# Splitting queries and keys before they are turned, and turning them by DMA, in a fused attention and expert kernel

## The chip, the cores and the metric

The kernel runs on one core of a Trainium2 chip. The metric is the device time of one execution in microseconds (us), the median of several runs. TensorE is called PE, VectorE DVE, ScalarE ACT, GpSimd POOL; SP is the queue from which every DMA of this kernel is issued.

## The reference

Attention with queries averaged in pairs (32 heads, 1,152 keys and 576 queries each, width 64), then a layer over 2,304 tokens:

```python
q_pool = q.reshape(B, H, S // 2, 2, D).mean(axis=3)          # B, H, S, D = 4, 8, 1152, 64
scores = np.matmul(q_pool, k.transpose(0, 1, 3, 2)) / np.sqrt(D)
attn = np.exp(scores - scores.max(-1, keepdims=True))
attn = attn / (attn.sum(-1, keepdims=True) + 1e-09)
x = np.matmul(attn, v)                                       # then heads beside each other: 2304 x 512
h = x @ w_in                                                 # 512 x 1024, inputs in float64
sm = softmax(h); solu = h * sm
ln = (solu - mean) / np.sqrt(var + 1e-06) * g_ln
out = ln @ w_out                                             # 1024 x 512
```

## The kernel before

Every factor of a product is split into a float16 high part and a float16 low part, and the products of the parts are added in PSUM. Heads are taken in 16 pairs P; a head g has nine steps, each 128 keys against all 576 queries, 288 steps in all. A step is two score products for each half of the queries (`q,w` and `q,w2h` in the trace; pair 0 works in float32, `q,w2f`), an exponential on ACT, and the product with the values, five matmuls of 128 queries by 65 columns for each pair of parts. `eh` holds the exponentials' high part; a second exponential on ACT in float32 (`e32`, `e` in the trace) and a subtraction on POOL (`rest`, line 1104) give the low part beside it. For steps that the table `EX` picks (`whole`), ACT writes float32 alone, nothing is subtracted, and the five matmuls take float32 exponentials and float32 values (`vx`): one matmul in the program, two in the trace.

Ahead of a head's steps, `maxima` (line 944) multiplies queries by keys once more in 128 x 384 pieces, and DVE reduces each piece (`mx`, line 960) to find the shift of the exponentials.

`pair` (line 600) brings in queries, keys and values of a pair. Before the change PE turns nine 128 x 128 blocks of keys (`kt`, line 716) and five of queries (`qt`, line 802) per pair; ACT writes the high part from PSUM (`khi`, `q`), DVE the low part (`klo`, `q`, line 444, from PSUM); then plain DMAs put high and low parts beside each other (`k_put`, line 733; `q_beside`, line 823). The two expert weights come in 16 parts of 128 x 512, read as 64-bit words and made into float32 by ACT, POOL and DVE (`weight_part`), and split by `weight_split`: high on ACT, low on DVE (`wil`, `wol`). From step 78 on, 18 tiles of 128 tokens go through `tokens` (line 1234) between the steps.

The order on each engine is that of a planner (`Plan`): each operation is handed in with a wanted time `at`, counted in steps, an engine and a length; `run` plays these through and fixes the order. The numbers in `KP` set the wanted times and which steps take which path.

## Time and profile before

| | |
|---|---|
| median of 3 runs (lowest to highest) | 713.29 us (713.26 to 714.19) |
| the profiled execution: its time / its span | 713.3 us / 711.5 us |
| mean granted clock of PE | 0.97 |
| busy: PE / DVE / ACT / POOL | 651.9 / 561.8 / 560.7 / 491.0 us |
| HBM read / written | 36.70 / 4.72 MB |

Busy time is the union of an engine's spans; a matmul's span is longer than the distance to the next one, so what a matmul costs PE is read from start to start. The first scores start near 22.6 us of the span, head 2 near 67.4, head 4 near 100.3, head 8 near 180.3, head 9 near 201.5, and head 31 near 614.1.

### The profile page before, as it was taken

The numbers are of one execution on the slowest core, as the hardware profiler recorded it, in microseconds if no ns is written. First come the engines' busy times: TensorE is split into PE (matmuls) and PEld (weight loads), VectorE is DVE, ScalarE is ACT, GpSimd is POOL, SyncE is SP. The second block draws the span as 40 slices with busy tenths as digits, with TensorE's granted clock in tenths as the row PEclk, the third lists the DMA queues.
The fourth block names the chain that finished last, engine by engine and source line by source line (L and its number), as shares of the span: only waits on it lengthen the run. The fifth ranks groups of instructions, "written<-read, shape, count | busy, mean of one in ns | idle before, by whom it ended". The sixth has DMA issues, their size and how long they took to land.

```text
span 711.5 us, 19079 instructions
## 1 busy us (share of the span) xinstructions
PE 651.9 (92%) x7109; PEld 458.7 (64%) x7109; DVE 561.8 (79%) x1421; ACT 560.7 (79%) x1346; POOL 491.0 (69%) x643
## 2 busy tenths in 40 slices
PE   8879898677788999999999999999999999999995
PEld 7767676556555666676666666667767666665542
DVE  6689999998998888888888778797888786445551
ACT  3768789778879898899888887898989887864432
POOL 3575769776787978788878887778778787840100
PEclk9889999879989999999999999999999999999998
DMA  6664645442333333323423241423242201010101
GB/s 180 146 169 117 171 114 132 127 115 74 90 78 85 76 86 93 82 62 111 93 75 84 78 99 52 117 60 95 72 101 74 70 11 25 17 23 16 28 17 30
DMA packets 81048, 59.52 MB, mean 84 GB/s; under 512 B 64572, under 2 KB 64572, under 8 KB 80956
## 3 DMA queue, kind: packets, MB, share of 16 engines
q1 hardware_dynamic: 80956, 58.31, 32.5%
q8 instruction: 55, 0.90, 0.5%
q14 instruction: 37, 0.30, 0.1%
HBM read 36.70 MB, written 4.72 MB: 58 GB/s over the span
## 4 chain that ended last, share of the span: by engine, by line
PE 39%; DVE 10%; ACT 6%; issue 2%; POOL 2%; ACTq 0%; POOLq 0%; DVEq 0%
PE bank L438 35%; DVE mx L960 3%; PE bank L1343 2%; ACT e L1081 2%; DVE q L444 2%; ACT eh L1081 2%; ACT q L812 1%; POOL eh L1104 1%; DVE e L1293 1%; ACT e L1286 1%; DVE st L1274 1%; PE bank L1254 1%; PE bank L716 1%; POOL st L1326 1%; DVE e L1330 0%
## 5 line engine op out<-in xcount | busy, mean ns | idle before, releaser
L1104 POOL TENSOR_TENSOR eh<-e,eh 128x512 f16<-128x512 f32 (+1 forms) x491 | 394.2, 828 | 117.0 <-ACT e L1087 30.6
L960 DVE TENSOR_REDUCE mx<-bank 128x1 f32<-128x384 f32 x420 | 219.1, 547 | 35.0 <-PE bank L438 33.3
L1081 ACT ACTIVATE e<-bank 128x288 f32<-128x288 f32 x426 | 177.1, 428 | 10.0 <-POOL eh L1104 5.5
L1081 ACT ACTIVATE eh<-bank 128x288 f16<-128x288 f32 x384 | 160.1, 425 | 29.4 <-PE bank L438 27.0
L438 PE MATMUL bank<-q,w 128*128 128x288 f16 (+1 forms) x576 | 165.6, 296 | 5.4 <-ACT e L1087 2.5
L438 PEld LDWEIGHTS <-eh 128*128 128x128 f16 x3924 | 142.5, 100 | 19.4 <-issue 7.7
L438 PE MATMUL bank<-q,w2h 65*128 65x288 f16 x540 | 153.3, 292 | 0.0
L438 PE MATMUL bank<-w,q 128*128 128x384 f16 (+1 forms) x390 | 122.1, 336 | 32.7 <-DVE mx L960 16.4
L438 PE MATMUL bank<-vhi,eh 128*128 128x65 f16 x2544 | 143.8, 197 | 1.8 <-DVE x L1160 1.7
L438 PE MATMUL bank<-vlo,eh 128*128 128x64 f16 x1380 | 140.8, 196 | 0.0
L438 PEld LDWEIGHTS <-w 128*128 128x128 f16 x540 | 53.5, 99 | 46.0 <-issue 20.7
L438 PEld LDWEIGHTS <-w2h 65*128 65x128 f16 x540 | 53.3, 99 | 40.8 <-issue 13.3
L1087 ACT ACTIVATE eh<-bank 128x576 f16<-128x576 f32 (+1 forms) x75 | 48.8, 657 | 11.8 <-PE bank L438 11.5
L438 PEld LDWEIGHTS <-q 128*128 128x128 f16 x360 | 35.4, 100 | 29.8 <-DVE q L444 7.7
L1326 POOL TENSOR_TENSOR st<-st 128x1 f32<-128x1 f32 x54 | 11.6, 215 | 60.4 <-ACT junk L1313 58.6
L444 DVE SCALAR_TENSOR_TENSOR q<-bank,qs,q 64x192 f16<-64x192 f32 (+2 forms) x120 | 38.7, 362 | 12.2 <-ACT q L812 8.6
L1087 ACT ACTIVATE e<-bank 128x576 f32<-128x576 f32 x63 | 41.4, 658 | 0.7 <-DVE eh L1104 0.4
L812 ACT ACTIVATE q<-bank,qs 64x384 f16<-64x384 f32 (+2 forms) x60 | 29.8, 496 | 6.6 <-PE bank L802 4.2
L1274 DVE TENSOR_REDUCE st<-bank 128x1 f32<-128x512 f32 x36 | 24.7, 685 | 11.3 <-PE bank L438 10.8
L719 ACT ACTIVATE khi<-bank,qs 128x384 f16<-128x384 f32 x45 | 27.2, 604 | 4.8 <-PE bank L716 3.6
L438 PE MATMUL bank<-wil,xh 128*128 128x512 f16 x104 | 30.7, 378 | 0.0
L438 PE MATMUL bank<-wih,xh 128*128 128x512 f16 x104 | 30.6, 384 | 0.0
(167 smaller groups left out, 1160.6 us busy)
## 6 DMA issues: line engine op xcount, KB each, us to landing
qt<-in_q_dram SPq DMA_DIRECT2D x16, 576.0 KB
kt<-in_k_dram SPq DMA_DIRECT2D x32, 288.0 KB
vt<-in_v_dram SPq DMA_DIRECT2D x14, 576.0 KB
out_dram<-o SPq DMA_DIRECT2D x36, 128.0 KB
w<-khi SPq DMA_DIRECT2D x30, 144.0 KB
w<-klo SPq DMA_DIRECT2D x30, 144.0 KB
w2h<-w SPq DMA_DIRECT2D x30, 144.0 KB
raw<-in_moe_w_in_dram SPq DMA_DIRECT2D x8, 511.6 KB
```

The lines of the kernel that those rows point to most:

```text
L438: nc.tensor.matmul(out=o, lhsT=a, rhs=b, start=first, stop=last, skip_group_check=True)
L444: nc.vector.scalar_tensor_tensor(out=o, in0=a, scalar=scale, in1=b, op0=ALU.mult, op1=ALU.subtract)
L716: nc.tensor.transpose(ps[:, c, :], tl["kt", P][:, 3 * i + c].rearrange("p h d -> p (h d)"), ident)
L719: nc.scalar.activation(out=tl["khi", P][:, 3 * i:3 * i + 3], in_=tl["kps", (P, i)], func=ACTF.Copy, scale=tl["qs", P][:, 2:3])
L812: nc.scalar.activation(out=tl["q1", P][r, :, t, :], in_=ps, func=ACTF.Copy, scale=tl["qs", P][r, 1:2])
L960: nc.vector.tensor_reduce(out=tl["mx", g][:, m, c:c + 1], in_=tl["nps", (g, m, c)], op=ALU.max, axis=AXX)
L1081: nc.scalar.activation(out=tl[name, (g, j)][:, f * HALF:(f + 1) * HALF], in_=tl[tn(j, f), (g, j, f)], func=ACTF.Exp, scale=esc,)
L1087: nc.scalar.activation(out=new((name, (g, j)), [128, SQ * 4 // mybir.dt.size(dtype)], dtype)[:, 0:SQ].rearrange("p (f i) -> p f i", f=2), ...
L1104: eng.tensor_tensor(out=e[:, o:o + c.stop - c.start], in0=e32[:, c], in1=e[:, c], op=ALU.subtract)
L1274: nc.vector.tensor_reduce(out=st(f), in_=tl[H_[f]], op=ALU.max, axis=AXX)
L1326: nc.gpsimd.tensor_tensor(out=st(o), in0=st(a), in1=nhalf if b is None else st(b), op=op)
L1343: nc.tensor.transpose(ps[:, c, :], tl[E][:, o:o + 128], ident)
```

## The change

Queries and keys of pairs 1 to 15 are split as they lie, in SBUF: ACT writes the high part, DVE the low part, into one tile in which high and low alternate (`kn`) or in two (`qa`, in which POOL copies the high part a second time beside itself, and `qb`). Six DMA transposes per pair, two of 128 x 1152 and four of 64 x 1152 float16, bring the turned parts where the products want them. The PE transposes, the reads of PSUM and the plain DMAs that set parts beside each other are gone; a plain DMA copies the high keys of each head to `khi`. The weights' first product writes to PSUM, and their low part is formed against a copy of the high part that PE puts into PSUM (`ups`); the float32 weights and their two parts share a tile. All values are loaded into two fixed float32 tiles. `EX` goes from 12 float32 steps (steps 10 to 34) to 31, every second one from 10 to 70. `OFF` adds an offset to the wanted time of each operation, and `KP` has new numbers.

```diff
-KP = {'W': [2, 4.42, 4.58], 'step': 1.32, 'M': [78.27, 16.0, 7.69], 'TX': 115, 'TP': 75, 'win': 5.1, 'P': [25.14, 18.81, 12.42, 24.66, 30, 23.73], 'QP': 27, 'N': [11.54, 7], 'AV': 4.37, 'CD': [[19, 71, 1], [71, 283, 10]], 'SD': [[11, 74, 2], [79, 283, 0]], 'VM': 'BBCCACBCBACCABBA', 'AH': 8, 'OF': [4.15, 1.91, 9.71, 2.05, 1.96], 'N1': 10.15, 'warm': 1, 'ws': 1.98, 'GR': 1, 'GG': 19, 'b_eh': 6, 'b_w1': 4, 'V0': -54.65, 'VF': 1, 'QD': [0, 1], 'L0': 0.56, 'F': 0, 'EX': [[10, 36, 47]], 'LX': [0, 23.98], 'HP': [146073, 0], 'DL': 2000, 'MA': 17.97, 'WS': [50, 75, 1.36]}
+KP = {'W': [2, 4.44, 4.7], 'step': 1.05, 'M': [78.33, 15.88, 7.65], 'TX': 118, 'TP': 69, 'win': 4.28, 'P': [24.74, 18.81, 12.81, 18.34, 35, 22.83], 'QP': 29, 'N': [11.98, 7], 'AV': 5.18, 'CD': [[27, 53, 2], [69, 288, 10]], 'SD': [[12, 83, 5], [70, 287, 1]], 'VM': 'BACCBCACBCCBCACB', 'AH': 8, 'OF': [4.76, 1.62, 9.84, 2.47, 1.86], 'N1': 8.51, 'warm': 1, 'ws': -3.83, 'GR': 0, 'GG': 13, 'b_eh': 6, 'b_w1': 4, 'V0': -98.83, 'VF': 1, 'QD': [0, 1], 'L0': 2.74, 'F': 0, 'EX': [[10, 71, 50], [42, 282, 0]], 'LX': [3, 36.19], 'HP': [146073, 0], 'DL': 2000, 'MA': 18.0, 'TR': [2000, 2], 'P1': [-3.89, -3.14, 3.71, -7.84, -10.1, 0.03], 'WS': [47, 70, 0.22], 'KD': 5.48, 'KL': 0, 'WP': 0}
+OFF = {'am.0': -3.59, 'am.1': 4.37, 'am.10': -9.61, 'am.11': -5.09, 'am.12': -8.44,
...
+        at += OFF.get(self.group((writes or reads)[0]), 0)
...
-    tag(1, "kt")
+    tag(2, "kt")
...
         def product():
+            ps = psum(("wps", n), WN)
             nc.vector.tensor_scalar(
-                out=w32.bitcast(I32), in0=tl["raw", n][:, :, 0], scalar1=5, scalar2=128 << 23,
+                out=ps.bitcast(I32), in0=tl["raw", n][:, :, 0], scalar1=5, scalar2=128 << 23,
                 op0=ALU.logical_shift_right, op1=ALU.bitwise_or,
             )
-            nc.vector.tensor_tensor(out=w32, in0=w32, in1=tl["up", n].bitcast(F32), op=ALU.mult)
+            nc.vector.tensor_tensor(out=w32, in0=ps, in1=tl["up", n].bitcast(F32), op=ALU.mult)
...
-        add("DVE", DVE(WN) + 4, at + 0.3, lambda: left(lo, w32, scale, hi), [*need, (dst[m], 0, n)], [(dst[m], 1, n)])
+        def again():
+            mm(psum(("ups", n), WN), id16, hi, True, True)
+
+        add("PE", MH(WN), at + 0.2, again, [(dst[m], 0, n)], [("ups", n)], kind="long")
+        add("DVE", DVE(WN) + 68, at + 0.3, lambda: left(lo, w32, scale, tl["ups", n]), [*need, ("ups", n)], [(dst[m], 1, n)])
...
+        def k_hi():
+            o = new(("kn", P), [128, 2, NJ, 2, D], F16)[:, :, :, 0, :].rearrange("p h j d -> p j h d")
+            nc.scalar.activation(out=o, in_=tl["kt", P], func=ACTF.Copy, scale=tl["qs", P][:, 2:3])
+
+        def k_lo():
+            t = tl["kn", P]
+            for h in range(2):
+                left(t[:, h, :, 1, :], tl["kt", P][:, :, h, :], tl["qs", P][:, 2:3], t[:, h, :, 0, :], low_eng)
+
+        def k_turn(h):
+            g = 2 * P + h
+            o = new16(("w1", g), 128, S).rearrange("p (j c) -> p j c", j=NJ)
+            nc.sync.dma_start_transpose(out=o, in_=tl["kn", P][:, h].rearrange("p j r d -> p (j r d)"))
...
+        def q_lo2():
+            left(qb[P % 2][:, :, 0, :], q_nat(), tl["qs", P][:, 1:2], tl["qa", P][:, :, 0, :])
+
+        def q_twice():
+            t = tl["qa", P]
+            nc.gpsimd.tensor_copy(out=t[:, :, 1, :], in_=t[:, :, 0, :])
...
+            nc.sync.dma_start_transpose(
+                out=tl[k, P][:, h], in_=t[D * h:D * h + D].rearrange("p t r d -> p (t r d)")
+            )
```

On SP, where pair 2 (heads 4 and 5) is made ready; `w_866` and `w_904` before, `w_941` and `w_970` after, are these heads' keys, `q_868`, `q_884` and `q_924` the queries. Before:

```order
L733 DMA w_866<-khi 64x1152
L733 DMA w_866<-klo 64x1152
L733 DMA w_904<-khi 64x1152
L733 DMA w_904<-klo 64x1152
L501 DMA raw<-in_moe_w_in_dram 128x4093
L1062 DMA w2h_83<-w_621 64x1152
L615 DMA qt<-in_q_dram 128x1152
L823 DMA q_868<-q_868 64x5x64 x2
L823 DMA q_868<-q_868 64x4x64 x2
```

With the change:

```order
L804 DMA_TRANSPOSE q_884<-qa 128x9x64 x2
L804 DMA_TRANSPOSE q_924<-qb_85 128x9x64 x2
L720 DMA_TRANSPOSE w_941<-kn 128x9x128
L720 DMA_TRANSPOSE w_970<-kn 128x9x128
L632 DMA vx_81<-in_v_dram 128x9x64 x2
L512 DMA raw<-in_moe_w_in_dram 128x4093
```

Eight plain copies between tiles give way to six transposes, with the loads of values and weights queued behind them.

On PE in the middle of the program, at the queries of one pair (`qt`) between the maxima (`w,q`) and a token tile's second product (`lh`). Before:

```order
L802 MATMUL bank<-ident,qt 128x128 x3
L438 LDWEIGHTS q_4805
L438 MATMUL bank<-w_4810,q_4805 128x384
L438 LDWEIGHTS lh
L438 MATMUL bank<-wol,lh 128x512
L438 LDWEIGHTS lh
L438 MATMUL bank<-wol,lh 128x512
L802 MATMUL bank<-ident,qt 128x128 x2
```

With the change no such rows are left after pair 0. In head 4, where float16 parts alone stood before, PE now has float32 value products and the copy of a weight part (`id_66`):

```order
L447 MATMUL bank<-q_924,w2h_80 128x288
L447 LDWEIGHTS q_1407
L447 MATMUL bank<-w_1485,q_1407 128x384
L447 MATMUL bank<-vx_81,eh 128x65 x5
L447 LDWEIGHTS id_66
L447 MATMUL bank<-wb_67,id_66 128x512
```

The five float32 matmuls stand in place of fifteen float16 ones; 14 transposes per pair are gone.

On DVE among the token tiles, at the keys' low part (`klo`, `kn`), between reductions of maxima (`mx`). Before:

```order
L960 TENSOR_REDUCE mx<-bank 128x1
L444 SCALAR_TENSOR_TENSOR klo<-bank,qs,khi 128x384
L960 TENSOR_REDUCE mx<-bank 128x1 x2
L1221 TENSOR_SCALAR xs<-xs 128x1
```

With the change:

```order
L941 TENSOR_REDUCE mx<-bank 128x1 x5
L453 SCALAR_TENSOR_TENSOR kn<-kt,qs,kn 128x9x64 x2
L941 TENSOR_REDUCE mx<-bank 128x1
```

Three instructions that read PSUM, apart from each other, become two that read SBUF twice and stand back to back.

## Rows read from the trace of the kernel before

**Rows 1.** The page's second part: PE's granted clock in 40 slices, in tenths.
```profile
PEclk9889999879989999999999999999999999999998
```

**Rows 2.** Two stretches: us, busy (instructions) per engine, clock, DMA share, GB/s.
```profile
22.60:201.50 178.90, 144.22 (x1645) 113.10 (x1644) 163.67 (x354) 145.74 (x260) 131.31 (x100) 0.90 0.51 129
201.50:614.10 412.60, 398.24 (x4733) 278.43 (x4732) 337.28 (x921) 362.80 (x978) 330.81 (x474) 1.00 0.30 75
```

**Rows 3.** Second score products alone (`w2h`, two per step): PE, PEld, POOL, clock, DMA.
```profile
67.40:100.30 32.90, 9.86 (x37) 3.50 (x36) 0.00 (x0) 1.00 0.58 153
100.30:180.30 80.00, 21.55 (x72) 7.67 (x72) 0.00 (x0) 0.89 0.45 116
```

**Rows 4.** Float32 values (`vx`) alone: PE, PEld, ACT, POOL, clock, DMA.
```profile
67.40:100.30 32.90, 8.77 (x71) 8.50 (x70) 0.00 (x0) 0.00 (x0) 1.00 0.58 153
100.30:180.30 80.00, 2.45 (x20) 2.50 (x20) 0.00 (x0) 0.00 (x0) 0.89 0.45 116
```

**Rows 5.** Heads 2 and 3, and heads 4 to 7, all engines as in rows 2.
```profile
67.40:100.30 32.90, 28.88 (x325) 23.37 (x323) 31.35 (x69) 26.26 (x46) 22.18 (x16) 1.00 0.58 153
100.30:180.30 80.00, 62.11 (x799) 47.50 (x797) 75.10 (x159) 66.15 (x115) 63.12 (x46) 0.89 0.45 116
```

**Rows 6.** Costliest groups, DVE, ACT and POOL: busy us, mean ns of one; idle before.
```profile
L444 DVE SCALAR_TENSOR_TENSOR q<-bank,qs,q 64x192 f16<-64x192 f32 (+2 forms) x120 | 38.7, 362 | 12.2 <-ACT q L812 8.6
L522 DVE TENSOR_TENSOR wi<-wi,up 128x512 f32<-128x512 f32 x8 | 10.2, 1273 | 0.8
L1293 DVE SCALAR_TENSOR_TENSOR e<-bank,xs,e 128x512 f32<-128x512 f32 x26 | 19.3, 745 | 3.8 <-ACT e L1286 3.5
L1087 ACT ACTIVATE e<-bank 128x576 f32<-128x576 f32 x63 | 41.4, 658 | 0.7 <-DVE eh L1104 0.4 <-POOL eh L1104 0.3
L1104 POOL TENSOR_TENSOR eh<-e,eh 128x576 f16<-128x576 f32 x59 | 81.2, 1388 | 37.7 <-ACT e L1087 27.0 <-PE bank L438 6.2 <-DVE mx L960 3.4
```

**Rows 7.** DVE low parts, `klo` alone from PSUM: ns min/median/max, first and last start.
```profile
L444 DVE SCALAR_TENSOR_TENSOR klo<-bank,qs,khi x45: 591/608/618, 31.4 to 549.8; 128x384 f16<-128x384 f32 x45
L444 DVE SCALAR_TENSOR_TENSOR wil<-wi,ws,wih x8: 751/1283/1762, 125.1 to 156.5; 128x512 f16<-128x512 f32 x8
L444 DVE SCALAR_TENSOR_TENSOR wol<-wo,ws,woh x8: 732/806/1725, 191.7 to 213.2; 128x512 f16<-128x512 f32 x8
L908 DVE SCALAR_TENSOR_TENSOR vlo<-vt,vs,vhi x4: 1412/1508/1985, 167.0 to 577.5; 128x1152 f16<-128x1152 f32 x4
```

**Rows 8.** PE's timeline near 90 and 94 us: start us, us, what.
```profile
90.28 1.23 PE L438 MATMUL bank<-vx,eh 128*128 128x65 f32 x10
91.34 0.33 PE L438 MATMUL bank<-w,q 128*128 128x384 f16 x1
91.51 0.49 PE L716 MATMUL bank<-ident,kt 128*128 128x128 f32 x3
91.83 0.29 PE L438 MATMUL bank<-q,w 128*128 128x288 f16 x1
...
93.46 0.19 PE L438 MATMUL bank<-vhi,eh 128*128 128x65 f16 x1
...
94.36 0.52 PE L716 MATMUL bank<-ident,kt 128*128 128x128 f32 x3
```

**Rows 9.** PE transposes of keys, then of queries, in one stretch: PE, PEld.
```profile
201.50:614.10 412.60, 14.92 (x90) 11.04 (x90) 1.00 0.30 75
201.50:614.10 412.60, 8.83 (x50) 6.29 (x50) 1.00 0.30 75
```

**Rows 10.** PE's waits over the whole span: us in total, times, longest.
```profile
PE bank L438 <- DVE mx L960: 19.3, 25, 2.8
PE bank L438 <- DVE q L444: 9.2, 14, 2.9
```

**Rows 11.** DMA packets of SP's queue; then SP's issues of two copies, ns min/median/max.
```profile
q1 hardware_dynamic: 80956, 58.31, 32.5%
L823 SPq DMA_DIRECT2D q<-q x60: 590/615/1399, 39.9 to 566.4; - x60
```

More of the change, by code (lines that the diff above doesn't have):

```diff
@@ L569, in weight_split @@
     def weight_split(n, at, i, f, m):
-        c = slice(f * WN, (f + 1) * WN)
-        dst = "wi", "wo"
-        w32, hi, lo = (x[m][:, i, c] for x in ((wi32, wo32), (wih, woh), (wil, wol)))
+        dst, j = ("wi", "wo"), n % 8
+        w32, hi, lo = wb[m][:, j + 1], w16[m][:, j, 0], w16[m][:, j, 1]
         scale = ws[m][:, 8 + i:9 + i] if m else ws[m][:, 3:4]
@@ L753, in prep_k0, with prep_k @@
             add("DVE", DVE(PW) + 4, at, lambda: k_lo0(i, h), [ps, hi], [lo])
-        def prep_k(i, at):
-            ps, hi, lo = ("kps", (P, i)), ("khi", P, i), ("klo", P, i)
-            add("PE", TR(3), at, lambda: k_tr(i), [KT], [ps], also=[hi, lo], kind="whole")
-            add("ACT", ACT(PW, 1), at, lambda: k_hi(i), [ps, ("qs", P, 1)], [hi])
-            add("DVE", DVE(PW) + 4, at, lambda: k_lo(i), [ps, hi, ("qs", P, 1)], [lo])
-            if i == 2:
-                for h in range(2):
-                    for l in range(2):
-                        add("SP", DMA(64 * S * 2, 200), at + 4 * h + 0.5, lambda h=h, l=l: k_put(h, l),
-                            [("klo" if l else "khi", P)], [("w1", 2 * P + h, l)])
+        def prep_k(at):
+            S_, KN, G = ("qs", P, 1), ("kn", P), 2 * P
+            KD = 0.1 if P == 1 else KP["KD"]
+            add("ACT", ACT(2 * SQ, 1, 1), at, k_hi, [KT, S_], [(*KN, 0)])
+            add(*(("DVE", 2 * DVE(SQ) + 636) if P >= KP["KL"] else ("POOL", 2 * POOL(SQ))), at, k_lo, [KT, S_, (*KN, 0)], [(*KN, 1)])
+            for h in range(2):
+                add("SP", TRD, at + KD * h + 0.5, lambda h=h: k_turn(h), [KN], [("w1", G + h, 0)], calls=TRC)
+            for h in range(2):
+                add("SP", DMA(64 * S * 2, 200), at + KD * h + 0.55, lambda h=h: k_stack(h), [("w1", G + h)], [("khi", P, h)])
         def q_tr(i):
@@ L819, in q_beside, with q_nat, q_hi2 @@
-        def q_beside(odd):
-            r, o = (slice(D, 2 * D), slice(0, D)) if odd else (slice(0, D), slice(D, 2 * D))
-            for h in range(2):
-                t = tl["q1", P][:, h, odd:NT:2, :]
-                nc.sync.dma_start(out=t[o], in_=t[r])
+        def q_nat():
+            return tl["qt", P].rearrange("p t r d -> p (t r d)")[:, 0:SQ].rearrange("p (t d) -> p t d", t=NT)
+        def q_hi2():
+            o = new(("qa", P), [128, NT, 2, D], F16)[:, :, 0, :]
+            nc.scalar.activation(out=o, in_=q_nat(), func=ACTF.Copy, scale=tl["qs", P][:, 1:2])
@@ L850, in pair @@
             for i in range(3):
+                prep_k0(i, 0, at_k[i], [])
+            for i in range(3):
                 prep_q(i, at_q + i * 0.1)
         VM = KP.get("VM", "BBBBBAAAAAAAAAAA")[P]
-        if VM == "A" and P < VX:
+        if VM == "A":
             VM = "C"
@@ L1025, in maxima @@
             return first()
-        todo = [(m, c) for m in ((0, 4, 1, 2, 3) if nm == 5 else range(4)) for c in range(3)]
+        todo = [(m, c) for m in (range(5) if nm == 5 else range(4)) for c in range(3)]
         for i, (m, c) in enumerate(todo):
@@ L1197, in scores @@
                         add("PE", 5 * 218 * len(js1), a + KP.get("AV", 2), lambda js=js1: values(js),
-                            [*need, ("vx", 0, P % 2, "v"), ("vx", 0, P % 2, "one")], [("av", g)], kind="whole")
+                            [*need, ("vx", P % 2, "v"), ("vx", P % 2, "one")], [("av", g)], kind="whole")
                     elif js1:
@@ L1378, in tokens @@
             last_f = f"f{i}"
-        add("DVE", DVE(DF, 1) + 64, a + 2 + KP.get("NO", 0), norm, P_("mean", "f4"), [(*E, 0), (*E, 1)])
+        add("DVE", DVE(DF, 1) + 250, a + 2 + KP.get("NO", 0), norm, P_("mean", "f4"), [(*E, 0), (*E, 1)])
         if prev is not None:
```

167 lines of the change are left out of this document (61 added, 106 removed).

## The prediction

> **What bounds the kernel now.** I read the clock by slices first, then the busy times of long stretches, then the pace of the steps, and last the single groups. The clock [rows 1] shows two programs in one: up to the twelfth slice it drops to 0.7 or 0.8 again and again, which means that PE had idled and was put to its lower level (1.2 in place of 2.4 GHz) for part of the time; after that it stays near full. Two stretches say why [rows 2]. From 22.6 to 201.5 us (heads 0 to 8) DVE is busy 163.67 of 178.9 us, 91%, and PE 81% at a clock of 0.90: there DVE sets the pace, with ACT at 81% and POOL at 73% behind it. From 201.5 to 614.1 us (heads 9 to 30, with the token tiles) PE is busy 398.24 of 412.6 us, 97%, DVE 82%, ACT 88%, POOL 80%: there PE sets it. The reader is to see that the same microsecond of work is worth something on another engine in each.
>
> Within the first stretch the pace is uneven. Heads 2 and 3 have 36 second score products, 18 steps, in 32.9 us; heads 4 to 7 have 72, 36 steps, in 80.0 us [rows 3]: 1.83 against 2.22 us a step. What differs is the float32 steps: heads 2 and 3 have eight of the 18, and their window holds seven steps' worth of float32 values (71 pieces, ten a step); heads 4 to 7 have none, and their window only two steps' worth left over from head 3 (20 pieces) [rows 4]. In heads 4 to 7 DVE is busy 75.10 of 80.0 us, and POOL rises from 22.18/32.9 to 63.12/80.0, 67 to 79% [rows 5].
>
> **What the change does to heads 1 to 8.** The float32 steps go from 12 to 31; heads 4 to 7 get 18 of their 36, as dense as heads 2 and 3 have now. Each saves a second exponential on ACT, 658 ns, and a subtraction on POOL, 1,388 ns [rows 6]. Each costs PE more: ten float32 pieces take 91.34 - 90.28 = 1.06 us, while thirty float16 ones, two steps, take 94.36 - 93.46 = 0.90 us, 0.45 a step [rows 8]. So 0.61 us more for each of 19, 11.6 us of PE, in a stretch where PE has 178.9 - 144.2 = 34.7 us free [rows 2]; I cost it at nothing, because DVE covers it. Without that cover it is 11.6 us.
>
> DVE then has to follow. Per weight part, the product now reads one factor from PSUM. With both in SBUF it took 1,273 ns; the row with one factor in PSUM and one float32 in SBUF, of the same size, took 745 [rows 6]. I take 745, 0.53 us less (bounds: 0 if the wait is not of that kind, 0.53). Eight such parts fall in heads 4 to 7 (by `W` the ninth is wanted at step 2 + 8 x 4.44 = 37.5, the last at 70): 4.2 us. The low parts of the first weight matrix have a median of 1,283 ns with a least of 751 [rows 7], and will read PSUM: 8 x 0.53 = 4.3 us. PE's copies for it, 16 matmuls of 512 columns, are new; three matmuls of 128 columns take 0.32 us [rows 8] in float32, so 16 matmuls of 512 columns cost at most 16 x 0.43 = 7 us, and lie in PE's free time.
>
> Queries' and keys' low parts cost three `klo` of 608 ns [rows 7] and eight `q` of 362 [rows 6], 4.7 us a pair, and become three instructions of 576 elements that read two SBUF tiles. No row has that form; the nearest are the weights' (512 elements) and the values' (1,152) [rows 7]. Scaled to 576, the least is 1,412/2 = 0.71 us and the most 1,762 x 576/512 = 1.98 us, so 2.1 to 5.9 us a pair. I take 1.0 us each (between the medians 0.75 and 0.91 of `vlo` and `wol`, with a little for the early rows at 1.44), 3.0 us a pair, 1.7 less. The spread from 751 to 1,762 ns of one form means that such an instruction sometimes waits for something. The Trainium skill (SBUF — State Buffer, Two separate sides) says that a VectorE operation with two SBUF inputs and a GpSimd operation that reads SBUF exclude each other for a whole instruction; the trace agrees as far as `klo`, with one operand in PSUM, stays between 591 and 618 ns [rows 7], and by that rule alone the price would be the least, 0.71 us, or that and the rest of a POOL instruction of up to 1.4 us, and the sum would stay inside the same bounds.
>
> Together heads 4 to 7 lose 4.2 + 4.3 + 2 x 1.7 = 11.9 us of DVE's 75.1: 63.2 us, 1.76 a step, about what heads 2 and 3 have (31.35/18 = 1.74 [rows 5]). Two ways thus give the pace of heads 2 and 3: 36 steps x 1.83 = 65.9 in place of 80.0, **14 us less**. Heads 1 to 3 keep their float32 density and gain only some DVE time, where PE is already busy 28.88 of 32.9 us: 1 us. Head 0 and head 8 I leave as they are. First stretch: -15 us (0 to -25).
>
> **What it does to heads 9 to 30.** PE loses 90 transposes of keys and 50 of queries there [rows 9]. Three of them take 0.32 us from start to start [rows 8], 0.11 each: 140 x 0.11 = **15.3 us less** on the engine that is busy 97%. ACT loses its reads of PSUM and gains two longer ones; POOL gains ten copies of 576 elements and reads of `v` that went to DVE before, and has 82 us free there [rows 2]. DVE changes by 10 x (-1.7). What is late next is ACT at 88%, which must not rise above PE: it does not, since it loses work per pair too. The tail after 614 us holds no queries or keys and stays. The start stays too: pair 0 is prepared as before.
>
> **The transposes.** Six per pair replace eight copies on SP; no row shows one. Each K transpose moves 295 KB, each Q transpose 147 KB. If they go as packets of 256 bytes at the mean time of a packet, 0.325 x 16 x 711.5/80,956 = 46 ns [rows 11], that is 1,152 x 46/16 = 3.3 us and 1.7 us, 13 us of all DMA engines for a pair that has 2 x 412.6/22 = 37.5 us; with the 30 to 50% that they do now [rows 2] it fits. If each element of 2 bytes were a packet, 147,456 x 46/16 gives 424 us for a K transpose, and the kernel would run for milliseconds. I take the low end, since the plain copies between tiles are issued in 0.6 us [rows 11] and never show up as a wait of PE. Queued behind them on SP are the loads of values and weights.
>
> **Sum.** Against the profiled execution's 713.3 us, which is the median of the runs (713.29): 713.3 - 15 - 15.3 = 683.
>
> **Rivals.**
> *The transposes become the bound* (slower). Mechanism: SP's transposes and the tiles behind them finish at a rate below one pair in 37.5 us; `w,q` and `q,w` wait, and PE's clock falls. It decides from about 9 us per K transpose (two K and four half as long make a pair's 37.5 us). At 11.8 us it is 4 x 11.8 = 47 us a pair: beginning near 25 us, fifteen pairs until 25 + 15 x 47 = 730, then head 30 in 18.8 us and the 97 us from head 31 to the end: about 847 us. For it: nothing in the trace gives a transpose's rate. Against it: DMA has half its time free. The Trainium skill (VectorE: DVE Perf Modes, The three transpose paths) puts a DMA transpose of 128 x 128 at 1,309 ns against 390 on TensorE, and its rule is to use TensorE where PSUM will do; by that figure nine blocks give the 11.8 us. Another page (Advanced Engine Details and Errata, X-Bar Transpose) calls them as fast as plain DMAs, by which they hide. No run so far shows either.
>
> *One of the two gains fails.* In heads 4 to 7 the clock of 0.89 [rows 5] stays low and float32 values, at half rate 2.1 us, make PE the bound; or in heads 9 to 30 two back-to-back `kn` of up to 2 us each hold up the maxima, on which PE already waits 19.3 us [rows 10], and 1.5 us a pair eat the 15. Either gives 698.
>
> *More than that.* PE waits 19.3 us for maxima and 9.2 us for queries' low parts [rows 10]; parts made early by DMA end the second, and a clock that stays full helps the first: up to 20 us more, 663.
>
> *Nothing comes of it*: both gains fail, 713.
>
> **Chances.** As forecast (672 to 692) 0.55; one gain fails (692 to 711) 0.18; more (655 to 672) 0.11; nothing 0.03; transposes bound 0.09, and other losses (DMA waits in the early heads, new order worse) 0.04, above 715. A difference under 0.2%, 1.4 us, can hardly be told from none here. Faster 0.84, same 0.03, slower 0.13. With 0.13 above and a few in a hundred below and between, 660 to 708 holds eight in ten; the forecast's own range is 672 to 692.
>
> **What would show it.** Right: head 8 starts near 165 us, the clock in heads 4 to 7 is near 1.0, steps there take 1.8 us; heads 9 to 30 take near 397 us with no `kt` or `qt` on PE and no wait of `q` or `w` on a DMA. Wrong: PE waits on `q<-qa`, `w<-kn` or `kn`; `kn` near 2 us; SP issues transposes for most of the span.

## The result, and the profile after

The changed kernel takes **656.37 us** (median of 4 runs, 655.9 to 656.55) where the kernel before took 713.27 on the same chip: a ratio of 0.9211 [0.9176, 0.9247]. The forecast was 683 us, with 660 to 708 for its range. The direction was right, but the gain is 57 us, not 30, and the time lies below the range. In the profiled execution (655.9 us, span 654.1) it lies here, by the first score product of each head:

| stretch | before, us | after, us | difference | forecast |
|---|---|---|---|---|
| start, to head 0 | 22.6 | 22.7 | +0.1 | 0 |
| head 0 | 29.1 | 24.6 | -4.5 | 0 |
| heads 1 to 3 | 48.6 | 45.9 | -2.7 | -1 |
| heads 4 to 7 | 80.0 | 61.9 | -18.1 | -14 |
| head 8 | 21.2 | 17.5 | -3.7 | 0 |
| heads 9 to 30 | 412.6 | 388.0 | -24.6 | -15.3 |
| head 31 and tail | 97.4 | 93.5 | -3.9 | 0 |

The clock by slices (answers to [rows 1]): after the third slice it stays at 0.9 or above, and the drops to 0.7 and 0.8 are gone but for one.

```profile
PEclk9979999999999999999999999999999999999999
```

The windows of the two stretches (heads 0 to 8, heads 9 to 30; they answer to [rows 2]), then heads 2 and 3 and heads 4 to 7 ([rows 5]): start and end, length, busy time of PE, PEld, DVE, ACT and POOL, clock, DMA share, GB/s.

```profile
22.70:172.60 149.90, 136.27 (x1506) 111.98 (x1505) 140.00 (x315) 126.23 (x223) 107.60 (x87) 0.98 0.75 165
172.60:560.60 388.00, 375.52 (x4577) 262.25 (x4575) 323.30 (x846) 345.40 (x927) 354.92 (x480) 1.00 0.49 100
62.20:93.20 31.00, 28.72 (x332) 24.45 (x331) 28.59 (x66) 24.61 (x40) 19.94 (x15) 1.00 0.81 188
93.20:155.10 61.90, 58.20 (x639) 47.46 (x637) 58.52 (x136) 53.86 (x93) 41.60 (x32) 1.00 0.78 172
```

The float32 value pieces (tile `vx`) in heads 4 to 7 ([rows 4]); the first busy time is PE's:

```profile
93.20:155.10 61.90, 21.33 (x170) 20.70 (x170) 0.81 (x1) 6.09 (x7) 4.76 (x2) 1.00 0.78 172
```

Heads 4 to 7 now run like heads 2 and 3: DVE has gone from 75.10 to 58.52 us and POOL from 63.12 to 41.60. PE does more float32 work (170 pieces in that window, 20 before) but is *less* busy, 58.20 in place of 62.11: its clock is 1.00 in place of 0.89, and 28 transposes, 5.5 us of busy time in the trace of before, are gone. In heads 9 to 30 PE lost 398.24 - 375.52 = 22.7 us of busy time, and ACT lost 362.80 - 345.40 = 17.4 too [rows 2]; the second number is the one that the forecast didn't use.

DVE's low parts of keys, weights and queries (one line of a helper; ns min/median/max, first and last start), which answer to [rows 7]:

```profile
L453 DVE SCALAR_TENSOR_TENSOR kn<-kt,qs,kn x30: 799/814/1902, 28.6 to 510.0; 128x576 f16<-128x576 f32 x30
...
L453 DVE SCALAR_TENSOR_TENSOR wb<-wb,ws,bank x16: 705/736/749, 111.4 to 185.4; 128x512 f16<-128x512 f32 x16
L453 DVE SCALAR_TENSOR_TENSOR qb<-qt,qs,qa x15: 796/1233/1824, 31.2 to 500.6; 128x576 f16<-128x576 f32 x15
```

The weights' product from PSUM, in the same columns:

```profile
L534 DVE TENSOR_TENSOR wb<-bank,up x16: 690/692/692, 24.8 to 153.8; 128x512 f32<-128x512 f32 x16
```

What reads PSUM has no spread (690 to 692, 705 to 749); what reads two SBUF tiles still has (796 to 1,902).

The DMA transposes as SP issues them, in the same columns (the keys' row, then the queries'):

```profile
L720 SPq DMA_TRANSPOSE w<-kn x30: 1258/1314/2472, 32.1 to 512.9; - x30
```

```profile
L804 SPq DMA_TRANSPOSE q<-qa x30: 1199/1263/1771, 30.6 to 508.1; - x30
L804 SPq DMA_TRANSPOSE q<-qb x30: 1209/1262/2777, 33.5 to 514.3; - x30
```

PE's waits over the whole span (answer to [rows 10]: maxima 19.3 us before, low parts of queries 9.2); none is on a DMA:

```profile
PE bank L447 <- DVE mx L941: 6.5, 13, 1.5
PE bank L447 <- ACT e L1062: 5.5, 14, 0.7
PE bank L447 <- DVE wb L534: 3.0, 4, 1.1
```

### The profile page after: what moved, and what is told of

The parts are those of the page before. It is cut to its first block, busy times and chain, and to the rows that moved or that the text cites. A ratio compares the mean times of both kernels' runs of the same rounds, so it can differ in the third digit from the quotient of the medians.

```text
span 654.1 us, 18337 instructions
## 1 busy us (share of the span) xinstructions
PE 619.2 (95%) x6847; PEld 442.5 (68%) x6847; DVE 523.2 (80%) x1308; ACT 524.6 (80%) x1262; POOL 493.8 (75%) x640
## 4 chain that ended last, share of the span: by engine, by line
PE 56%; DVE 8%; ACT 4%; POOL 3%; issue 2%; ACTq 0%; DVEq 0%
PE bank L447 52%; POOL eh L1085 3%; DVE mx L941 3%; PE bank L1323 2%; ACT e L1062 1%; PE bank L1235 1%; ACT eh L1062 1%; DVE st L1254 1%; DVE vx L877 1%; DVE eh L1075 1%; DVE e L1273 1%; ACT e L1266 0%; DVE eh L1085 0%; DVE ll L450 0%; PE bank L950 0%
## 5 line engine op out<-in xcount | busy, mean ns | idle before, releaser
L1085 POOL TENSOR_TENSOR eh<-e,eh 128x512 f16<-128x512 f32 (+1 forms) x467 | 371.3, 821 | 57.2 <-ACT e L1068 13.2
L447 PEld LDWEIGHTS <-eh 128*128 128x128 f16 x3639 | 130.8, 98 | 21.1 <-issue 3.5
L447 PE MATMUL bank<-vhi,eh 128*128 128x65 f16 x2354 | 132.8, 195 | 2.7 <-POOL eh L1085 2.3
L447 PE MATMUL bank<-wb,xh 128*128 128x512 f16 x208 | 59.5, 378 | 0.2 <-ACT eh L1062 0.2
L447 PE MATMUL bank<-wb,lh 128*128 128x512 f16 x208 | 58.2, 378 | 0.3 <-DVE e L1273 0.3
L1068 ACT ACTIVATE eh<-bank 128x576 f32<-128x576 f32 (+1 forms) x69 | 44.3, 656 | 16.2 <-PE bank L447 16.2
L893 POOL TENSOR_TENSOR vlo<-vx,vhi 128x1152 f16<-128x1152 f32 x16 | 38.5, 2409 | 6.9 <-ACT vhi L884 6.7
L447 PEld LDWEIGHTS bank<-vx,eh 128*128 128x128 f32 x310 | 37.8, 192 | 1.4 <-DVE x L1141 0.8
L447 PE MATMUL bank<-vx,eh 128*128 128x65 f32 x310 | 38.7, 272 | 0.1
L526 POOL TENSOR_TENSOR up<-up,un 128x512 f32<-128x512 f32 x16 | 21.7, 1359 | 18.6 <-DVE mx L996 7.9
L1254 DVE TENSOR_REDUCE st<-bank 128x1 f32<-128x512 f32 x36 | 24.5, 681 | 9.6 <-PE bank L447 9.3
```

The costliest lines, as they stand in the source:

```text
L447: nc.tensor.matmul(out=o, lhsT=a, rhs=b, start=first, stop=last, skip_group_check=True)
L526: nc.gpsimd.tensor_tensor(out=up, in0=up, in1=tl["un", n].bitcast(F32), op=ALU.subtract)
L893: nc.gpsimd.tensor_tensor(out=o, in0=t, in1=h, op=ALU.subtract)
L1068: nc.scalar.activation(out=new((name, (g, j)), [128, SQ * 4 // mybir.dt.size(dtype)], dtype)[:, 0:SQ].rearrange("p (f i) -> p f i", f=2), ...
L1085: eng.tensor_tensor(out=e[:, o:o + c.stop - c.start], in0=e32[:, c], in1=e[:, c], op=ALU.subtract)
L1254: nc.vector.tensor_reduce(out=st(f), in_=tl[H_[f]], op=ALU.max, axis=AXX)
```

## The experiments

**The theories.** A, the forecast's: the float32 steps and the weights free DVE, ACT and POOL in heads 0 to 8, and PE's lost transposes shorten heads 9 to 30; only the sizes were off. B: the missing 27 us are the offsets of the due times (the second half of the new table). C: the DMA transposes hide no better than they must, and cost something already. D to H stand in the texts below. Times in the tables are stretches of the profiled execution; ratios are against the kernel before, run on the same chip.

### The offsets, and the float32 steps

The first run empties the table:

```diff
-OFF = {'am.0': -3.59, 'am.1': 4.37, ...}
+OFF = {}
```

> The changed kernel with the table of offsets emptied, so that the planner goes by its formulas alone; every operation stays. Theory A (the operations themselves give the gain; the offsets are a trim): 656 to 672 us, with heads 4 to 7 at 62 to 66 us and heads 9 to 30 at 388 to 398 us. Theory B (the 27 us that the forecast missed are the offsets'): 680 to 686 us, with heads 9 to 30 back at some 397 to 405 us, the start or the tail longer, and the wait of PE on the row maxima back near 19 us.

Measured: 665.9 us, 0.9358 [0.9314, 0.9402]. Heads 0 to 8 and heads 9 to 30, windows as above:

```profile
23.50:176.10 152.60, 138.64 (x1503) 111.81 (x1502) 140.52 (x315) 126.04 (x223) 109.02 (x87) 0.97 0.72 159
176.10:569.20 393.10, 379.34 (x4571) 262.16 (x4572) 325.17 (x844) 347.13 (x926) 352.15 (x480) 1.00 0.49 99
```

Rival B falls as the cause of all 27 us: the offsets are worth 664.3 - 654.1 = 10.2 us of span, of them 2.7 in heads 0 to 8, 5.1 in heads 9 to 30, 1.6 in the tail and 0.8 in the start. That is a term of its own, though, which the forecast did not have. All further variants are made from this run ("without offsets"), except where the text says otherwise.

Then the steps, in the changed kernel and in the kernel before:

```diff
 # the changed kernel
-'EX': [[10, 71, 50], [42, 282, 0]]
+'EX': [[10, 36, 47]]
 # the kernel before
-'EX': [[10, 36, 47]]
+'EX': [[10, 71, 50]]
```

> The changed kernel with 12 float32 value steps as before instead of 31; the 19 others go back to weights and values in two float16 parts, with one ACT and one POOL operation more for each. Theory A (the float32 steps free ACT, DVE and POOL in heads 4 to 7, where PE waits for them): heads 4 to 7 go from 61.9 back to 72 to 78 us with a clock near 0.9, heads 9 to 30 stay within 3 us of 388, total 666 to 673 us. Rival D (the float32 steps give nothing, and the heads gain by the weights' shorter operations and by the transposes that left PE): 654 to 660 us.

> The kernel before with 31 float32 value steps instead of 12, and nothing else. Theory A: heads 4 to 7 fall from 80.0 to some 66 to 70 us and heads 9 to 30 stay at 412 us, total 699 to 704 us. Rival D (nothing by the float32 steps alone): 711 to 716 us.

Measured: 689.47 us (0.9677 [0.9635, 0.9718]) for the changed kernel with 12 steps, 33 us lost, more than either theory gave; and 712.98 (1.0019 [0.9991, 1.0047]) for the kernel before with 31, **nothing gained**. The same steps are worth 33 us in one kernel and none in the other. The window of heads 4 to 7 in the kernel before with 31 steps:

```profile
99.60:182.70 83.10, 71.93 (x686) 59.85 (x684) 70.41 (x158) 57.61 (x98) 41.56 (x30) 0.86 0.43 114
```

POOL went from 63.12 [rows 5] to 41.56 us and ACT from 66.15 to 57.61, as the forecast says, and DVE from 75.10 to 70.41, so that no engine but PE is above 85% of the 83.1 us. But PE's work grew: at a clock of 0.86 the longer value products make it 71.93 us busy in place of 62.11, 9.8 us more, while its idle time fell by only 6.7 (17.9 to 11.2). The order of that kernel had been made for 12 steps; whether due times of its own would let it gain was not tried.

The 33 us mix the steps' worth with an offset table made for 31 of them; hence the same without offsets:

> The changed kernel with 12 float32 value steps as before and with the offsets emptied, beside the run with 31 steps and without offsets (665.9 us). If the 33 us that 12 steps cost with the offsets were half a misfit of a table made for 31 steps, it comes out at 675 to 682 us. If they are the steps' own worth, 690 to 699 us. If the offsets alone are what makes the steps pay, 664 to 669 us.

Measured: 676.85 us (0.9475 [0.9439, 0.9512]). So the steps are worth 11 us (9.5 of them in heads 0 to 8, 162.1 against 152.6), and the table that gains 10 us with 31 steps *loses* 12.6 with 12: it fits one set of operations only. The first of the three answers was right. All runs here keep the other numbers of the new `KP`, which were made for 31 steps and the detour of the weights below; what numbers of its own would give each variant was not tried.

### Do the steps pay by the clock?

At those 26 of the 31 places that take float16 parts again, idle PE work is put back, for the run with 12 steps, with offsets and then without:

```diff
+def idle(j):
+    ps = psum(("dps", (g, j)), 4, 128)
+    for c in range(5):
+        nc.tensor.transpose(ps[:, c % 4, :], ident, ident)
```

> The changed kernel with 12 float32 value steps as before, and at each of the 31 steps' places that are now in float16 five idle 128x128 float32 transposes on PE whose results nothing reads (0.55 us, about what a float32 step adds to PE). Theory A (the float32 steps pay by what they take off ACT, DVE and POOL): 686 to 700 us, as without the idle work or worse. Rival G (they pay because they keep PE busy and its granted clock at full speed): clock of heads 4 to 8 at 0.98 and up, total 656 to 675 us.

> The run with 12 float32 steps and without offsets (676.9 us, clock 0.97) with five idle 128x128 float32 transposes on PE at each of the 31 places: the earlier run with idle work again, without the table that fits neither. Theory A (the float32 steps pay by what they take off ACT, DVE and POOL): 675 to 686 us. Rival G (they pay by PE's activity and clock): 664 to 670 us, heads 4 to 7 near 65 us at a clock of 0.97 and up.

Measured: 683.45 us (0.9584 [0.9563, 0.9605]) and 678.67 (0.9517 [0.9484, 0.955]). Without offsets the whole run's clock goes from 0.971 to 0.990, heads 4 to 7 from 72.9 to 69.8 us, heads 9 to 18 from 179.7 to 181.5, and the total does not move. Heads 4 to 7 with idle work, without offsets and then with them:

```profile
96.70:166.40 69.70, 61.11 (x831) 48.19 (x829) 61.87 (x137) 61.47 (x105) 59.98 (x46) 0.98 0.70 161
```

```profile
92.30:172.40 80.10, 65.66 (x834) 50.72 (x832) 66.08 (x143) 64.74 (x108) 60.17 (x46) 0.94 0.71 156
```

Rival G falls for the total: an active PE gives back at most 3 of the 7.7 us that heads 4 to 7 lack (65.2 with 31 steps). With offsets the total did fall, by 6.0 us, but not by this: heads 4 to 7 took 80.1 in place of 73.2 us, and 4.8 of the gain lie in heads 9 to 30, where no idle work stands. Presumably the offsets fit the one order less badly than the other there.

### The weights by way of PSUM

```diff
-ps = psum(("wps", n), WN)      # takes one factor of the product, in PSUM
...
-nc.vector.tensor_tensor(out=w32, in0=ps, in1=tl["up", n].bitcast(F32), op=ALU.mult)
+nc.vector.tensor_tensor(out=w32, in0=w32, in1=tl["up", n].bitcast(F32), op=ALU.mult)
...
-left(lo, w32, scale, tl["ups", n])     # ups: the high part, copied to PSUM by a matmul
+left(lo, w32, scale, hi)
```

> The run without offsets (665.9 us, heads 0 to 8 in 152.6) with the weights' products made in place in SBUF and their low parts taken against the high parts in SBUF, as before: no detour by PSUM, no copying matmuls on PE. Theory A (the detour saves DVE 0.5 us for each of 16 products and 16 low parts, where DVE sets the pace): heads 0 to 8 at 160 to 168 us, the product near 1,270 ns, total 674 to 682 us. Rival H (DVE has room once the float32 steps and the transposes are there): heads 0 to 8 at 151 to 156 us, total 664 to 669 us.

> The run without offsets with 12 float32 steps and with the weights in SBUF throughout: neither of the two that act on heads 0 to 8, which took 152.6 us with both, 162.1 with the weights by PSUM alone and 174.7 with the float32 steps alone. If each acts by itself, the sum: 184 us, total 695 to 705 us. If the float32 steps pay only once DVE has been freed, as the run of the kernel before with 31 of them says: 173 to 178 us, total 686 to 693 us.

Measured: 691.21 us (0.9698 [0.9634, 0.9763]) with 31 steps, more than either answer gave, and 695.06 (0.9777 [0.9726, 0.9828]) with 12. With the two runs above this makes a square, heads 0 to 8 in us:

| | weights by PSUM | weights in SBUF |
|---|---|---|
| 31 float32 steps | 152.6 | 174.7 |
| 12 float32 steps | 162.1 | 177.1 |

The detour is worth 22.1 us with the float32 steps and 15.0 without; the steps 9.5 with the detour and 2.4 without. By the medians of the totals it is 25.3 and 18.2 for the detour, 11.0 and 3.9 for the steps. The executions with 31 steps and the weights in SBUF scatter from 687.8 to 697.8, so the steps' gain without the detour, 2.4 or 3.9, can't be told from none. The steps need the detour, the detour is worth more with the steps, and the weights are the larger part; the forecast had none of this. For "neither", the expected 173 to 178 us of the second answer came true (its total of 686 to 693 was 2 us short). Rival H falls. Heads 4 to 7 show how, in four runs without offsets (31 steps by PSUM, 12 by PSUM, 31 in SBUF, 12 in SBUF):

```profile
93.00:158.20 65.20, 60.10 (x639) 48.41 (x638) 59.97 (x138) 53.96 (x93) 41.78 (x31) 0.97 0.71 159
```

```profile
96.30:169.20 72.90, 61.27 (x754) 42.56 (x753) 65.56 (x144) 63.49 (x108) 62.37 (x47) 0.88 0.77 158
```

```profile
98.80:177.60 78.80, 68.39 (x659) 54.87 (x658) 68.51 (x139) 55.01 (x92) 43.16 (x32) 0.87 0.58 134
```

```profile
100.40:180.30 79.90, 59.61 (x727) 43.05 (x724) 77.19 (x143) 65.00 (x109) 67.12 (x47) 0.85 0.72 146
```

In the last DVE is 97% busy (77.19 of 79.9) and sets the pace. With float32 steps alone (third) DVE falls to 87%, but PE's clock is 0.87, its idle time 10.4 us (5.8 of it waits for row maxima), and at that clock its work has grown to 68.39 us. With the detour alone (second) DVE, ACT and POOL stand at 85 to 90% together. Only the first gets the clock back to 0.97, and then PE's own work shrinks by 8 us. The two rows of DVE with the weights in SBUF, product and low part:

```profile
L533 DVE TENSOR_TENSOR wb<-wb,up x16: 692/965/2684, 28.2 to 178.5; 128x512 f32<-128x512 f32 x16
```

```profile
L453 DVE SCALAR_TENSOR_TENSOR wb<-wb,ws x16: 730/910/2883, 113.2 to 200.2; 128x512 f16<-128x512 f32 x16
```

The least is near that of the PSUM form (690, 705); the median is a quarter to two fifths more and the longest four times as much. What they wait for can be read from the trace, one by one. The longest product, and what POOL did when it started:

```profile
83.03 2.68 DVE L533 TENSOR_TENSOR wb<-wb,up 128x512 f32<-128x512 f32 x1
```

```profile
82.60 2.57 POOL L888 TENSOR_TENSOR vlo<-vx,vhi 128x1152 f16<-128x1152 f32 x1
```

POOL's operation ends at 85.17 us, DVE's at 85.71, 0.54 later. So it is with all: ten of the 16 products start while an operation of POOL runs, and each of these ends 0.54 to 0.55 us after that operation; the six that start with POOL idle take 0.69 us. In the changed kernel 13 of the 16 start while POOL works, and all take 690 to 692 ns. The product with both operands in SBUF thus waits for the POOL operation that it meets, and with one operand in PSUM it does not. The Trainium skill (SBUF — State Buffer, Two separate sides) says that a VectorE operation with two SBUF inputs and a GpSimd operation that reads SBUF exclude each other for the whole instruction; the trace agrees.

PE's wait for the row maxima over the whole span, 19.3 us before [rows 10], goes with the weights too. With neither, with the float32 steps alone, and with the detour alone:

```profile
PE bank L447 <- DVE mx L936: 19.1, 17, 3.3
```

```profile
PE bank L447 <- DVE mx L936: 13.1, 14, 3.7
```

```profile
PE bank L447 <- DVE mx L941: 3.0, 7, 0.9
```

All three have the DMA transposes; only where DVE is rid of the weights' long SBUF operations do the maxima come in time.

### Heads 9 to 30: PE's transposes, keys, queries

First the whole old path of queries and keys, with its own due times, then its PE work alone (14 idle transposes a pair beside the new path):

```diff
+nc.tensor.transpose(ps[:, c, :], tl["kt", P][:, 3 * i + c]..., ident)   # and ACT and DVE read ps
-nc.sync.dma_start_transpose(out=o, in_=tl["kn", P][:, h]...)            # and 4 of queries
```

> The run without offsets (665.9 us) with the path of queries and keys of before put back for pairs 1 to 15: transposes on PE, parts read from PSUM, plain DMAs, and the due times of before for it. Theory A (the transposes are worth what PE issues for them, and the low parts' 1.7 us a pair of DVE): heads 9 to 30 grow from 393.1 by 15 us to 406 to 411, total 680 to 688 us. Rival E (their place in the order also makes PE wait for the maxima and for the q parts): heads 9 to 30 grow by 20 us or more to 413 and up, with PE's wait on mx near 15 us and on q near 9 us again, total 690 us and up. Rival F (the transposes were filling waits): total 666 to 672 us.

> The run without offsets (heads 9 to 30 in 393.1 us) with 14 idle 128x128 float32 transposes of the keys on PE for each pair 1 to 15, in groups of 3, 3, 3, 3 and 2, whose results nothing reads: the PE work of before alone, with no reads of PSUM. By the busy row of before (23.75 us for 140, 0.17 each): heads 9 to 30 at 416 to 421 us. By the forecast's 0.11 us each: 408 to 411 us. If PE's waits absorb part of them: under 405 us.

Measured: 698.79 us (0.9796 [0.9777, 0.9815]) and 686.11 (0.9625 [0.9595, 0.9654]). Heads 9 to 30 in the first and in the second:

```profile
182.80:600.40 417.60, 396.62 (x4716) 278.02 (x4715) 339.53 (x927) 363.88 (x978) 337.07 (x472) 1.00 0.34 73
```

```profile
183.60:587.60 404.00, 391.01 (x4680) 275.51 (x4678) 326.08 (x844) 349.65 (x927) 348.92 (x480) 1.00 0.47 95
```

The path is worth 417.6 - 393.1 = **24.5 us** here (and 6.2 in heads 0 to 8), as rival E's size has it. But its PE work alone is worth only 404.0 - 393.1 = **10.9**, the third answer: 140 transposes at 0.08 us, less than the forecast's 0.11 and half of the busy time that the trace of before puts down to them ([rows 9], 23.75 us). From start to start they still take 0.11 each, 15.4 us; the rest fell into PE's waits. (In heads 0 to 8 the idle transposes cost 8.4 us, no less than the whole path.) E's reason, waits of PE, fails too. In that stretch of the run with the whole old path PE waits this long for maxima and for parts of queries (us in total, times, longest):

```profile
PE bank L446 <- DVE mx L955: 4.0, 7, 0.9
PE bank L446 <- DVE q L452: 3.8, 8, 0.7
```

So something else cost 13.6 us, and the next two runs put back one path each:

> The run without offsets (665.9 us; heads 9 to 30 in 393.1) with the old path put back for keys alone (9 transposes a pair on PE, three reads of PSUM by ACT and three by DVE, four plain copies). Both paths back cost heads 9 to 30 24.5 us. If the cost goes by PE's busy time (15.0 of 23.4 us): 407 to 411 us here. If it is the queries' many small steps instead: 394 to 400 us. If either path alone costs nearly all, since both queue for the same three PSUM banks: 412 us and up.

> The run without offsets with the old path put back for queries alone (5 transposes a pair on PE, four reads of PSUM by ACT and eight by DVE, plain copies). If the cost goes by PE's busy time (8.4 of 23.4 us): heads 9 to 30 at 400 to 404 us. If it is the queries' many small steps: 407 to 415 us. If the keys' path is what costs: 393 to 397 us.

Measured: 678.62 us (0.9548 [0.9511, 0.9585]) for keys; 714.19 (0.9991 [0.995, 1.0033]) for queries, whose runs scatter from 706 to 715, with one of 726 and the profiled one at 706.6. Heads 9 to 30 with the keys', then with the queries' old path:

```profile
176.90:581.50 404.60, 388.37 (x4643) 271.43 (x4642) 327.65 (x861) 351.94 (x948) 346.99 (x481) 1.00 0.41 88
```

```profile
187.10:608.80 421.70, 393.89 (x4628) 270.76 (x4627) 346.35 (x918) 361.11 (x958) 344.05 (x472) 0.98 0.38 80
```

Keys cost 11.5 us for 90 transposes, and from start to start these take 10.6: there PE's time is nearly the whole price. Queries cost **28.6** for 50, which take 5.5. That is more than both paths together cost (24.5), and the total is longer too (714 against 699), so a part of it belongs to the order that the planner makes of this mixture, and the two prices can't be added. For the rest it is not PE: the queries' path puts 14 us on ACT and 21 on DVE (four reads of PSUM and eight, a pair) where the keys' puts 4.8 and 2.5. Does their number cost, or that PE waits for late queries? The last two runs add the steps beside the new path, where nothing waits for them:

```diff
+nc.tensor.transpose(flat(ps[:, c]), t[:, o:o + 128], ident)      # 5 a pair
+nc.scalar.activation(out=sp1[r, :, t, :], in_=ps, func=ACTF.Copy, scale=...)   # 4 a pair
+left(sp2[0:D, h, t, :], ps[:, h], ..., sp1[r, h, t, :])     # 8 a pair, left out in the second run
```

> The run without offsets (heads 9 to 30 in 393.1 us) with the queries' old steps beside the new path for pairs 1 to 15: 5 transposes on PE, 4 reads of PSUM by ACT and 8 by DVE a pair into spare buffers, whose results nothing uses; queries and keys still come by the DMA transposes. With the old path of queries in place of the new one the stretch took 421.7 us. If the small steps themselves cost (time on ACT and DVE, and PSUM banks held until both have read): 412 to 425 us. If it was PE waiting for late queries, and the steps are hidden: 395 to 403 us.

> The same without the 8 reads by DVE: 5 transposes on PE and 4 reads by ACT a pair. If what costs is PE and ACT: as the run before, within 5 us. If the DVE steps and the banks that they hold: 396 to 402 us for heads 9 to 30.

Measured: 702.64 us (0.9868 [0.9843, 0.9892]) and 692.08 (0.9716 [0.9675, 0.9757]). Heads 9 to 30 take 411.2 us with DVE's steps (just under the range of the first answer) and without them:

```profile
187.10:595.50 408.40, 388.44 (x4593) 266.56 (x4591) 322.94 (x845) 363.94 (x965) 352.50 (x480) 1.00 0.45 93
```

Five transposes and four reads by ACT a pair add 15.3 us, DVE's eight steps 2.8 more (in heads 0 to 8, where DVE has less room, 8.7 more: 172.5 against 163.8). At the 0.08 us of the run with idle transposes, 50 of them make 4, from start to start they take 6.7 here; the other 9 to 11 us go with 16.8 us that ACT gains in busy time (363.94 - 347.13), at 89% of the stretch. So **ACT's reads are probably the larger price**, though ACT is never the busiest engine here. That is a subtraction, and not shown: PE waits for exponentials of ACT only 1.7 us longer (6.7 against 5.0) and is 9.1 us longer busy, and the PSUM banks that are held until ACT has read them, or the new order, may be what costs. A run with ACT's reads from SBUF would tell. The rest of the 28.6 us is open: in that run the clock is 0.98 in place of 1.00, and its due times were those of before.

### Are the DMA transposes free?

```diff
 nc.sync.dma_start_transpose(out=o, in_=...)
+nc.sync.dma_start_transpose(out=o, in_=...)              # twice, same place
+nc.sync.dma_start_transpose(out=spare, in_=...)          # or into a spare buffer
+nc.sync.dma_start(out=spare, in_=...)                    # or two plain copies into spare buffers
```

These three are made from the changed kernel with its offsets.

> The changed kernel with each of its 90 DMA transposes issued twice, with the same data to the same place. Theory A (they lie beside other work): heads 9 to 30 within 3 us of 388, total 655 to 660 us, and SP issues transposes for twice as long. Rival C (they hold something up already, and the gain of the transposes that left PE is net of it): 90 more at 1.26 us of SP, or 13 us a pair of all DMA engines by the forecast's packet time, show as 10 us or more, total 666 us and up, with waits on a DMA or on w and q in the trace.

> The changed kernel with each of its 90 DMA transposes issued twice, the second one into a spare buffer that nothing reads and that is used again only two transposes later, so that SP doesn't wait for the first to land as in the run before (148 us of SP's waits stood there). If those waits made that run's 224 us: 656 to 675 us. If SP's issue time alone makes them (114 us more, in bursts of 12 that last 15 us and hold up all else that SP issues): 720 us and up, with PE waiting on a DMA.

> The changed kernel with two plain copies of the same source into spare buffers beside each DMA transpose, in place of the second transpose that cost 85 us: about the same issue time on SP (two of 0.6 us for one of 1.27) and twice the bytes, but no turning. If SP's issue time makes the 85 us: 725 to 750 us. If the turning itself, in the DMA engines, makes them: 656 to 675 us.

Measured: 880.59 us (1.2388 [1.2326, 1.245]), 741.36 (1.0388 [1.0346, 1.043]) and 742.14 (1.0378 [1.0314, 1.0443]). In the first, SP's waits show that the second copy waits for the first, each 1.6 us on the mean, which no theory had allowed for:

```profile
SPq L721 <- DMA w<-kn: 54.2, 30, 3.3
SPq L806 <- DMA q<-qb: 49.4, 30, 2.5
SPq L806 <- DMA q<-qa: 44.4, 30, 2.5
```

Without that wait 90 more transposes still cost 85 us of span (739.2 against 654.1), and **180 plain copies cost nearly the same, 82** (736.3; by the medians of the runs 85 and 86). The transposes into spare buffers (ns min/median/max; the last line is in us), then the plain copies:

```profile
L470 SPq DMA_TRANSPOSE spare<-kn x30: 1269/1355/2196, 35.3 to 600.1; - x30
...
DMA to landing us min/median/max: 2.6/3.0/3.9
```

```profile
L471 SPq DMA_DIRECT2D spare<-kn x60: 534/586/1263, 35.5 to 597.5; - x60
```

By the medians that is 30 x (1.268 + 1.355 + 1.276) = 117 us of SP in the one and 60 x (0.582 + 0.586 + 0.582) = 105 us in the other. So the turning itself is not what costs, and SP's time, in bursts, is near in both. PE's waits, in the same order:

```profile
PE bank L447 <- DMA w<-kn: 21.1, 8, 5.4
PE bank L447 <- DMA q<-c: 15.5, 6, 5.6
```

```profile
PE bank L447 <- DMA w<-kn: 22.5, 7, 7.1
PE bank L447 <- DMA q<-c: 10.4, 5, 6.3
```

Both wait alike, for `w` and for the small `q<-c` that stand behind the burst on SP. That the DMA engines are not the limit is likely and not shown: once issued, a transpose of keys lands after 3.1 us there (median, 5.3 at most), and their share in heads 9 to 30 is 0.60 and 0.66, against 0.49. The same copies from another engine's queue were not tried. Rival C falls for the kernel as it is, where PE waits for no DMA, but the room is less than one more burst. How much less was not tried.

### More float32 steps

The run without offsets with `'EX': [[10, 90, 50]]`. In heads 8 and 9 the closing sums take the last block of queries from another place than float32 steps put it, so this variant does not compute the attention of those heads; the work is the same in size, and only its time is used.

> The run without offsets (665.9 us) with the float32 steps going on at the same density to step 90 (40 in place of 31; head 8 and head 9 too). If ACT and POOL still bind there: 660 to 664 us. If PE does, at 0.6 us a step: 668 to 674 us.

Measured: 666.66 us (0.9379 [0.9335, 0.9423]), between the two answers and no different from 665.9; more steps gain nothing that can be seen. No run beat the changed kernel.

## Why the prediction was right in direction and short by 27 us

The step that failed is the first stretch's term, "-15 us (0 to -25)": it was 29.0 us (178.9 to 149.9), and 26.3 without offsets. The forecast took the weights' and the float32 steps' gain for two ways to one pace, left heads 0 and 8 as they were, and gave the new order no term. The runs show that the two edits are worth 24.5 us together, but 15.0 (the weights) and 2.4 (the steps) one by one, and the offsets 10.2 over the whole kernel.

The span fell by 57.4 us; the forecast had 30.3. Of the missing 27.1, the offsets make 10.2 and, without offsets, heads 0 to 8 make 11.3 (26.3 against 15), heads 9 to 30 4.2 (19.5 against 15.3) and the two ends 1.4 (2.3 in the tail, less 0.9 in the start).

- **Heads 4 to 7 at the pace of heads 2 and 3**: right. They take 1.72 us a step, 1.83 was expected, at a clock of 1.00, and head 8 begins at 155.1, not 165.
- **"Two ways thus give the pace"**, DVE's share or float32 density, was wrong as reasoning: neither way gives it alone. In heads 0 to 8 the float32 steps alone brought 2.1 us in the kernel before (178.9 to 176.8), the detour alone 15.0 (177.1 to 162.1), both 24.5. "I cost it at nothing, because DVE covers it": in heads 4 to 7 of the kernel before the steps cost PE 9.8 us, at a clock of 0.86, and the cover was not there. In the changed kernel it is: without offsets PE is 138.64 us busy in heads 0 to 8 with 31 steps and 138.45 with 12, at a clock of 0.97 in place of 0.89.
- **The weights, "4.2 us" and "4.3 us"** in heads 4 to 7: the term of the sum that was too small. The prices were right (692 and 736 ns against 745 and 751), and so was their sum: DVE's busy time there falls by 8.5 us (68.51 to 59.97). But the detour was worth 13.6 us of the stretch (78.8 to 65.2) and 8.5 in the other heads, since PE's busy time falls as well, by 8.3 at the higher clock, and all 16 parts reach from head 0 to head 8.
- **"Head 0 and head 8 I leave as they are"** failed: 4.5 and 3.7 us. Products of the weights start at 24.8 us and low parts run until 185.4; both heads are in their reach, and what else shortened them was not taken apart.
- **"140 x 0.11 = 15.3 us"** (the product is 15.4): the size was near, the reason was half of it. PE's transposes alone gave 10.9. The path gave 24.5, so what went with it (reads of PSUM by ACT and DVE, plain copies, the order) was worth the other 13.6. The step that failed here is "What is late next is ACT at 88%, which must not rise above PE": an engine at 88% was counted as free because another is at 97%. That ACT's part of the 13.6 is the larger is likely, as said above; the rest stays open. That the whole stretch gave 24.6 and the path 24.5 is partly chance: offsets gave 5.1 more, and the old operations under the new table's due times are slower (417.6) than under their own (412.6).
- **Queries' and keys' low parts, "3.0 us a pair"**: right. From the rows, 2 x 0.99 for `kn` and 1.20 for `qb` on the mean, 3.2. The forecast's price for one that waits for POOL, 0.71 + 1.4 = 2.1 us, lies a little outside its bound of 1.98, not inside as it says; the longest measured, 1,902 ns, lies inside.
- **Start and tail as before**: the start does; the tail gained 3.9 us, 1.6 of it by the offsets; the rest is open.
- **The transposes "as packets of 256 bytes", hidden**: right. The 90 into spare buffers bring 72,000 packets and 17.71 MB more, 246 bytes each. Six a pair take SP 1.3 us each, and PE waits for none. Rival 1's 11.8 us for a transpose of keys is far off. The Trainium skill's 1,309 ns for a block (VectorE: DVE Perf Modes, The three transpose paths) thus can't be taken nine times here: nine blocks are issued in 1.31 us, and those into spare buffers land 3.0 us after their issue.
- **What the forecast left out**: the due times. The sum put the order's own worth at nothing, and the chances had only "new order worse", at 0.04 with other losses; it was 10.2 us of gain for the offsets. What the other numbers of the new table are worth by themselves was not tried.

The likeliest case was thus right in direction and in where the gain lies, with terms too small, and wrong in how the two edits of the first stretch work on each other. That -15.3 came so near the 19.5 us of heads 9 to 30 without offsets is partly luck. Nearest in size was the rival "more than that" with 663 us, and its sign is there: of 28.5 us of waits for maxima and queries [rows 10] 6.5 are left. But its reason, parts made early by DMA, holds for the queries at most; the maxima's wait went with the weights.
